# Turning a tail row's last 64 keys on VectorE instead of TensorE, and four planned durations of a list scheduler

## The chip, the cores and the metric

The kernel runs on one core of one Trainium2 chip. The metric is the device time of one execution in microseconds, in which every engine, queue and transfer counts.

## What is computed

The reference is causal attention with a decay, followed by a two-layer feed-forward network with a leaky activation.

```python
batch, n_heads, seq, head_dim = (8, 8, 576, 64)
scores = (1.0 / np.sqrt(D)) * np.matmul(q, k.transpose(0, 1, 3, 2))
cum = np.cumsum(np.log(np.clip(f, 0.0001, 1.0)), axis=-1)
scores = np.where(causal, -1000000000.0, scores + cum[:, :, :, None] - cum[:, :, None, :])
attn = softmax(scores)
x = np.matmul(attn, v).transpose(0, 2, 1, 3).reshape(4608, 512)
h = x @ w_in                                   # 512 -> 2048
out = (np.maximum(h, 0.0) + alpha * np.minimum(h, 0.0)) @ w_out   # 2048 -> 512
```

## The kernel before

The work is cut into 32 pairs of heads, `n` = 0 to 31, four for each batch element; a pair has 576 queries and 576 keys for two heads. The query rows of a head are four tiles of 128 and a tail of 64; the tails of both heads lie together in one tile of 128 rows. For each tile TensorE makes scores, VectorE adds the decay and finds the extreme (L826, for tails L663), ScalarE takes the exponential (L620). For the multiplication with `v` the weights of attention must lie with keys on partitions, so they are turned.

Pairs 0 to 7 are turned block by block on TensorE with an identity matrix (L634, L864), and ScalarE or VectorE copies the result from PSUM. Pairs 8 to 31 are called turned (`turned`, `NX`): their exponentials go into one buffer of 3,136 columns, `rE`. VectorE turns its first 3,072 columns in 32x32 squares, in four instructions of 768 columns into four buffers `rM` (L838). Sixteen DMAs a pair (L842), of 32 partitions x 768 columns each, on SP's queue and on GpSimd's, put the squares in place in a buffer `rTT`. There are two of these, one inside the tensor `big`, one inside `wr` (`wf`), so the profile shows the pairs by turns as `big<-big` and `wr<-big`.

The last 64 columns of that buffer, 3,072 to 3,136, are the tail rows' weights for keys 512 to 575. Those are turned on TensorE: one transpose a pair (L674), kept in the list `tails` until the next pair's visit, then a copy by ScalarE into 64 partitions of `rT4` (`eT`, L672). The other 64 partitions of `rT4` are zeros. So the matmul with `v` for this chunk, number 4 in `prods_of`, has 128 rows, of which 64 are zeros.

A value block (`prods_of`, L906) multiplies all chunks of both heads with `v`; the two heads go to the two halves of the output's partitions side by side. Each of these float32 matmuls appears as two instructions. In `visit`, TensorE first does the tail transpose of the pair before and the value block of the pair two before, and then three stages of scores: tiles 0 and 1, tile 2, tile 3. The tail's scores are made in `tail`, in two parts of 256 and 320 keys. In pairs 0 to 7 `stretch` makes the scores.

While attention runs, TensorE also works on the first layer of the network for earlier batch elements: `ffn1`, matmuls `bank<-xx,wi` of 512 columns, called x matmuls below, six an operation.

The order on every engine is made when the program is built, by a list scheduler (`Plan`): each operation has a planned duration in ns, a key, dependences and buffers, and each engine takes the operation that can start first, the lower key among equals. On TensorE x matmuls have late keys and stand where attention, by the plan, must wait. The chip runs each engine's list in that fixed order. Up to 82 us of planned time, a wait planned for TensorE of over 0.5 us is filled with matmuls on the identity (`fill`, L475).

Planned durations of TensorE's operations: `c_mm(n)` is the larger of 110 and 13.3 + 0.4175 n; `c_row(n, m)` is m times that; a value block of a turned pair is `ns_v` = 2,517 ns.

Of the kernel before, what the change touches and what calls it, by code (L numbers as in the profile page):

```python
# [12 lines left out]
U64 = mybir.dt.uint64  # L13
# [12 lines left out]
EW = 3072 + 64  # L26
NN = 8
# [191 lines left out]
def attention_moe(  # L219
# [65 lines left out]
    big = sp.tile([128, EW + 2 * 3072], F32, name="big")  # L285
# [9 lines left out]
    wr = sp.tile([128, 1904], U64, name="wr")  # L295
# [4 lines left out]
    cq = wf[:, 3072 : 3072 + 16 * GN].rearrange("p (s g) -> p s g", g=GN)  # L300
    rT4 = ring(sp, 2, [128, 128], F32, "eT4_")
# [14 lines left out]
    selt = sp.tile([128, 768], F32, name="sel")  # L316
    sel = selt[0:9].rearrange("p (i n) -> p i n", n=128)
# [125 lines left out]
    def select():  # L443

        po.memset(sel, 0.0)
        for i in range(4):
            for h in range(2):
                po.affine_select(sel[:, i, 64 * h : 64 * h + 64], sel[:, i, 64 * h : 64 * h + 64], pattern=[[0, 64]], base=-(i + 5 * h),
                                 channel_multiplier=1, compare_op=ALU.not_equal, fill=1.0)
        for h in range(2):  # L450
            po.affine_select(sel[:, 4 + h, 64 * h : 64 * h + 64], sel[:, 4 + h, 64 * h : 64 * h + 64], pattern=[[0, 64]], base=-4,
                             channel_multiplier=1, compare_op=ALU.not_equal, fill=1.0)
# [130 lines left out]
    waiting, behind, tails, later_x, quick_ops, value_ops, turn_ops = [], [], [], [], [], [], []  # L583

    def attention(n):
# [24 lines left out]
        bT4, bst = Buf(rT4), Buf(rst)  # L610
# [31 lines left out]
        tail_64 = (lambda t: t[:, 3072:3136]) if turned else (lambda t: t[:, 512:S])  # L642
        cut = (lambda ap: ap.rearrange("p (j c) -> p j c", c=64)) if turned else (lambda ap: ap)

        def tail(st):
# [5 lines left out]
            for g in range(2):  # L651
# [8 lines left out]
                s = op("PE", nt_ * c_mm(w_), prods, st + 0.6 * g, rdy, [bS] + held)  # L660
# [29 lines left out]
        def quick(bR, r_, key):  # L690
# [4 lines left out]
            def prods():  # L695
                R9 = bR.t[0:9]
                for i in range(4):
                    mm(at(128 * i), sel[:, i], R9, True, True)
                mm(at(512), sel[:, 4], R9[:, 0:64], True, False)
                mm(at(512), sel[:, 5], R9[:, 64:128], False, True)  # L700
# [47 lines left out]
        def visit(st):  # L748
# [3 lines left out]
            bt_, nt_p, turn_tail, tail_done = tails.pop() if tails else (None, None, None, None)  # L752
            go = rdy
            if after or bt_:
                vb, vp, vd, done = after() if after else ([Buf(rS)], lambda: None, [], lambda o: None)
                b_ = vb[1] if after else vb[0]

                def begin():
                    if bt_:
                        turn_tail(b_)  # L760
                    vp()
# [3 lines left out]
                if bt_:  # L765
                    tail_done(b_, a)
                if after:
                    value_ops.append(a)
                    done(a)
                    plan.at("A", n)  # L770
# [11 lines left out]
        def stretch(tiles, st):  # L782
# [8 lines left out]
            ns = 340 + sum(c_row(128 * i + 128, nt_) for i in tiles) + (ns_v if after else 0)  # L791
# [585 lines left out]
```

## Time and profile before

| | us |
|---|---|
| median of three runs | 1007.79 |
| the three runs | 1007.56 to 1009.26 |
| the profiled execution | 1008.97 |
| span of its instructions | 1007.2 |

The span runs from the first to the last instruction; 1.8 us of the profiled execution lie outside it. The profiled execution is 1.18 us above the median of the runs. In rows of the trace PE is TensorE's matmuls, PEld its weight loads, DVE VectorE, ACT ScalarE, POOL GpSimd, SP SyncE, and SPq what SyncE's queue issues. A matmul's own duration holds its way through the array, which overlaps with the next ones; the distance between two starts is what it takes from TensorE.

### The profile page before, as it was taken

Reading aid. Unit: us, or ns where it says so; the run is one execution under the profiler, and the core shown is the slowest. Engines: PE = TensorE matmul, PEld = TensorE weight load, DVE = VectorE, ACT = ScalarE, POOL = GpSimd, SP = SyncE. Lnnn points to the kernel's source line nnn. Section 1 sums busy time; section 2 is a strip of 40 time slices with the busy share of each in tenths; the row PEclk is TensorE's granted clock in tenths of the full one; section 3 lists DMA queues with packets and bytes.
Section 4 is the critical chain, followed back from the end, with each engine's and each line's share of the span. In section 5 each row is a group of like instructions: output and inputs, shape, how many; then the busy total and the mean of one; then the engine's idle time right before and its main releaser. Section 6 shows DMA issues by size and latency. Waiting matters only on the chain.

```text
span 1007.2 us, 22383 instructions
## 1 busy us (share of the span) xinstructions
PE 999.4 (99%) x7828; PEld 878.8 (87%) x7828; DVE 804.5 (80%) x1730; ACT 643.4 (64%) x1534; POOL 371.7 (37%) x625
## 2 busy tenths in 40 slices
PE   9999999999999999999999999999999999999998
PEld 5777878888888888888888888999999999999998
DVE  6898788887878867867628966698898988989994
ACT  7878977887777677767446746564554645546551
POOL 5465877889778788666240000000000000000000
PEclk9999999999999999999999999999999999999999
DMA  7877868888888888777746664643434344434411
GB/s 213 257 213 241 261 222 240 244 246 259 250 244 266 249 251 241 220 221 210 208 150 230 201 222 146 208 138 120 152 120 134 119 141 133 133 117 135 140 50 43
DMA packets 129535, 191.04 MB, mean 190 GB/s; under 512 B 22647, under 2 KB 75886, under 8 KB 129422
## 3 DMA queue, kind: packets, MB, share of 16 engines
q1 hardware_dynamic: 124526, 175.24, 56.3%
q0 software_dynamic: 4608, 14.16, 5.3%
q8 instruction: 62, 1.02, 0.4%
q14 instruction: 51, 0.42, 0.1%
q10 hardware_dynamic: 288, 0.20, 0.1%
HBM read 102.95 MB, written 48.67 MB: 151 GB/s over the span
## 4 chain that ended last, share of the span: by engine, by line
PE 95%; DMA 2%; DVE 2%; ACT 1%; SPq 0%; issue 0%; DVEq 0%
PE bank L378 92%; PE bank L634 2%; DMA Z<-c8p 1%; DMA ri<-rd 1%; PE bank L441 1%; DMA rd<-R 0%; ACT big L620 0%; DVE xs L927 0%; PE bank L674 0%; DVE big L826 0%; DVE big L629 0%; PE bank L717 0%; SPq L730 0%; PE bank L475 0%; ACT big L630 0%
## 5 line engine op out<-in xcount | busy, mean ns | idle before, releaser
L378 PE MATMUL bank<-xx,wi 128*128 128x512 f32 x1728 | 407.8, 393 | 0.0
L378 PEld LDWEIGHTS bank<-xx,wi 128*128 128x128 f32 x1728 | 320.5, 188 | 68.8 <-issue 1.7
L620 ACT ACTIVATE big<-big,st 128x384 f32<-128x384 f32 (+4 forms) x272 | 158.0, 583 | 26.1 <-DVE st L826 23.8
L826 DVE CUSTOM_DVE_ANT_0 big<-bank,Z 128x384 f32<-128x384 f32 (+1 forms) x220 | 93.0, 480 | 54.2 <-PE bank L378 45.6
L378 PE MATMUL bank<-wot,xx 128*128 128x256 f32 x1008 | 123.9, 283 | 0.0
L378 PE MATMUL bank<-wi,xx 128*128 128x256 f32 x1008 | 123.9, 283 | 0.0
L378 PEld LDWEIGHTS bank<-wi,xx 128*128 128x128 f32 x1008 | 122.3, 192 | 0.0
L378 PEld LDWEIGHTS bank<-wot,xx 128*128 128x128 f32 x1008 | 122.3, 192 | 0.0
L1021 DVE SCALAR_TENSOR_TENSOR hs<-bank,sa,hs 128x512 f32<-128x512 f32 x96 | 71.4, 744 | 42.8 <-ACT hs L1019 41.4
L1019 ACT ACTIVATE hs<-bank,ab 128x512 f32<-128x512 f32 x96 | 65.8, 685 | 53.2 <-PE bank L378 52.0
L533 POOL TENSOR_TENSOR Z<-Z,tri 128x128 f32<-128x128 f32 x192 | 78.1, 437 | 44.8 <-DVE Z L509 35.7
L838 DVE STREAM_TRANSPOSE big<-big 128x768 f32<-128x768 f32 x96 | 88.6, 953 | 2.6 <-ACT big L620 2.5
L1261 ACT ACTIVATE xx<-gx 128x1024 fp32r<-128x1024 f32 x48 | 50.8, 1058 | 30.8 <-PE bank L378 15.1
L931 POOL TENSOR_TENSOR xx<-xs,xx 128x256 fp32r<-128x256 f32 x64 | 48.9, 783 | 49.9 <-ACT xx L929 49.4
L1264 DVE TENSOR_TENSOR xx<-gx,xx 128x1024 fp32r<-128x1024 f32 x48 | 58.6, 1220 | 7.5 <-ACT xx L1261 7.5
L378 PE MATMUL bank<-wi,gh 128*128 128x256 f32 x504 | 62.4, 283 | 0.0
L378 PE MATMUL bank<-wot,gh 128*128 128x256 f32 x504 | 62.4, 283 | 0.0
L378 PEld LDWEIGHTS bank<-wot,gh 128*128 128x128 f32 x504 | 61.4, 192 | 0.1
L378 PEld LDWEIGHTS bank<-wi,gh 128*128 128x128 f32 x504 | 61.3, 192 | 0.0
L378 PEld LDWEIGHTS bank<-big,vr 128*64 128x64 f32 x1088 | 51.9, 137 | 9.2 <-issue 4.8
L378 PE MATMUL bank<-big,vr 128*64 128x128 f32 (+2 forms) x1088 | 59.7, 263 | 0.0
L1016 ACT ACTIVATE hs<-bank,sg 128x512 f32<-128x512 f32 x48 | 33.1, 689 | 41.2 <-PE bank L378 32.2
(165 smaller groups left out, 1704.0 us busy)
## 6 DMA issues: line engine op xcount, KB each, us to landing
hd<-hs SPq DMA_DIRECT2D x144, 256.0 KB, 3.4
wx<-hd SPq DMA_DIRECT2D x47, 512.0 KB, 3.6
rqk<-in_qk_dram SPq DMA_DIRECT2D x28, 512.0 KB, 5.5
hr<-hd SPq DMA_DIRECT2D x25, 512.0 KB, 3.7
big<-big SPq DMA_DIRECT2D x120, 96.0 KB, 3.1
wr<-big SPq DMA_DIRECT2D x120, 96.0 KB, 3.9
vr<-in_vv_dram SPq DMA_DIRECT2D x32, 320.0 KB, 3.6
wr<-in_w_in_dram SPq DMA_DIRECT2D x16, 512.0 KB, 6.0
```

The lines of the kernel that those rows point to most:

```text
L378: pe.matmul(o, lhsT, rhs, start=start, stop=stop)
L533: ms.append(op("POOL", c_po(128), lambda to=to, i=i, zd=zd: po.tensor_tensor(to()[:, :, -1:], zd()[:, :, i : i + 1], tk(), ALU.add), kc + ...
L620: ex = op("ACT", c_exp(w), lambda: ac.activation(at(bt.t), at(bt.t), AF.Exp, bias=lo()[:, col : col + 1], scale=-1.0, accum_out=su()[:, co ...
L634: pe.transpose(t[:, c : c + 128], src[:, 128 * j : 128 * j + 128], ident)
L826: ve.tensor_tensor_reduce(out=o if turned else blk(o), in0=blk(bS.t[:, c0 : c0 + w]), in1=in1(), scale=-0.125, scalar=3.0e38, op0=ALU.add, ...
L838: tn = op("DVE", c_tr(768), lambda k=k: ve.transpose(part(bm[k].t), part(bE.t[:, 768 * k : 768 * k + 768])), k0 + TK + k / 10, done, [bE, ...
L931: xl = op("POOL", c_po(256), lambda r=r, t0=t0: po.tensor_tensor(bx.t[:, 1, t0 : t0 + 256], bxs[r].t[:, 0:256], bx.t[:, 0, t0 : t0 + 256]. ...
L1016: cp = op("ACT", c_act(512), lambda bh=bh, bs=bs, fc=fc: ac.activation(bs.t, bh.t, AF.Copy, scale=sg[:, fc : fc + 1]), -1000, [last, o_sg] ...
L1019: cp = op("ACT", c_act(512), lambda bh=bh, bs=bs, fc=fc: ac.activation(bs.t, bh.t, AF.Relu, scale=ab[:, fc : fc + 1]), -1000, [last, o_sg] ...
L1021: cp = op("DVE", c_dve(512), lambda bh=bh, bs=bs, fc=fc: ve.scalar_tensor_tensor(bs.t, bh.t, sa[:, fc : fc + 1], bs.t, ALU.mult, ALU.add), ...
L1261: his.append(op("ACT", c_acs(128 * GW * (j1 - j0)), lambda j0=j0, j1=j1, src=src, o_=o_: ac.activation(o_(0, j0, j1), src(), AF.Copy), key ...
L1264: rdy.append(op("DVE", c_dve(128 * GW * (j1 - j0)), lambda j0=j0, j1=j1, src=src, o_=o_: ve.tensor_tensor(o_(1, j0, j1), src(), o_(0, j0, ...
```

## The change

- The transpose on TensorE and the copy by ScalarE go, for all 24 turned pairs. Turned pairs take no `rT4` any more.
- VectorE turns the 64 columns with the rest: the third of the four instructions is followed by another of 32 columns (3,104 to 3,136), and the fourth is 800 columns wide instead of 768 (3,072 to 3,104 come last in it).
- The buffers `rM` and `rTT` are 800 and 3,200 columns wide (`MW`). Of the 16 DMAs of a pair, the eight of the third and fourth buffer bring 800 columns, the others 768 as before.
- The keys 512 to 575 of a tail now lie on partitions 64 to 127 of `rTT`. The matmuls of chunk 4 use these 64 rows only, and the rows 64 to 127 of `v`; `v`'s two halves of 32 rows change places in the input for turned pairs.
- `rT4` and a part of the selection matrix `sel` move into `big`, to make room.
- Four planned durations: a tail's scores get 60 ns more; a value block in `visit` 400 more, where before 120 stood for the transpose and any value block had its bare time; the three stages of scores in `visit` get 290, 0 and 110 in place of 340, 0 and 0; a `stretch` of scores in pairs 0 to 7 gets -100 in place of 340.

```diff
+MW = 768 + 32
-    big = sp.tile([128, EW + 2 * 3072], F32, name="big")
+    big = sp.tile([128, EW + 8 * MW], F32, name="big")
-    wr = sp.tile([128, 1904], U64, name="wr")
+    wr = sp.tile([128, 1968], U64, name="wr")
-    rT4 = ring(sp, 2, [128, 128], F32, "eT4_")
+    rT4 = Ring(Store(cuts_of(9024, 2, 128)))
-        bT4, bst = Buf(rT4), Buf(rst)
+        bT4, bst = None if turned else Buf(rT4), Buf(rst)
...
-                s = op("PE", nt_ * c_mm(w_), prods, st + 0.6 * g, rdy, [bS] + held)
+                s = op("PE", nt_ * c_mm(w_) + 60, prods, st + 0.6 * g, rdy, [bS] + held)
...
             if turned:
-                def tail_done(b_, o):
-                    nonlocal e4
-                    e4 = op("ACT", c_act(128), lambda: ac.activation(bT4.t[0:64], b_.t[0:64, 384:512], AF.Copy), st + 1.31, [o], [b_, bT4])
-
-                tails.append((bt, nt, lambda b_: pe.transpose(b_.t[0:64, 384:512], tail_64(bt.t), ident), tail_done))
                 return bt, nt
...
-            bt_, nt_p, turn_tail, tail_done = tails.pop() if tails else (None, None, None, None)
             go = rdy
-            if after or bt_:
...
-                a = op("PE", 120 + (ns_v if after else 0), begin, st, rdy + vd + ([nt_p, o_id] if bt_ else []),
-                       vb + ([bt_] if bt_ else []), need=(rS, len(vb[:2]) + 4))
...
+            if after:
+                vb, vp, vd, done = after()
+                a = op("PE", ns_v + 400, vp, st, rdy + vd, vb, need=(rS, len(vb[:2]) + 4))
...
-                s = op("PE", (340 if g == 0 else 0) + c_row(w_, nt_), lambda part=part: rows_of_scores(part), -3000, got, bS[g] + held, glue=1.5)
+                s = op("PE", (290, 0, 110)[g] + c_row(w_, nt_), lambda part=part: rows_of_scores(part), -3000, got, bS[g] + held, glue=1.5)
...
-            ns = 340 + sum(c_row(128 * i + 128, nt_) for i in tiles) + (ns_v if after else 0)
+            ns = (340 if n >= NN else -100) + sum(c_row(128 * i + 128, nt_) for i in tiles) + (ns_v if after else 0)
...
                     for k in range(4):
-                        tn = op("DVE", c_tr(768), lambda k=k: ve.transpose(part(bm[k].t), part(bE.t[:, 768 * k : 768 * k + 768])), k0 + TK + k / 10, done, [bE, bm[k]])
+                        w_ = MW if k >= 2 else 768
+
+                        def turn(k=k):
+                            c0, b_ = 768 * k, bm[k].t
+                            ve.transpose(part(b_[:, 0 : 768 if k < 3 else MW]), part(bE.t[:, c0 : c0 + (768 if k < 3 else MW)]))
+                            if k == 2:
+                                ve.transpose(b_[:, 768:MW], bE.t[:, 3104:3136])
+
+                        tn = op("DVE", c_tr(768) + (0, 0, 130, 33)[k], turn, k0 + TK + k / 10, done, [bE, bm[k]])
...
-                                bTT.t[32 * k : 32 * k + 32, 768 * a : 768 * a + 768], bm[k].t[32 * a : 32 * a + 32]), k0 + 8 + j / 100, [tn], [bm[k], bTT], kb=96))
+                                bTT.t[32 * k : 32 * k + 32, MW * a : MW * a + w_], bm[k].t[32 * a : 32 * a + 32, 0:w_]), k0 + 8 + j / 100, [tn], [bm[k], bTT], kb=w_ / 8))
...
-                                        + [(4, 256, 320, bT4.t[:, 64 * h : 64 * h + 64])] + [(j, 256, 320, tt_of(x3(j, 0), 2 * h, 2 * h + 2)) for j in range(4)])
+                                        + [(4, 256, 320, tt_of(768, 2 * h, 2 * h + 2)[64:128])] + [(j, 256, 320, tt_of(x3(j, 0), 2 * h, 2 * h + 2)) for j in range(4)])
...
-                        mm(o_.rearrange("p (a r) -> p a r", r=32) if len(m.shape) == 3 else o_, bv.t[:, j, h], m, c in first, c in last)
+                        mm(o_.rearrange("p (a r) -> p a r", r=32) if len(m.shape) == 3 else o_, bv.t[128 - m.shape[0] :, j, h], m, c in first, c in last)
...
-        if n == B * NP - 1:
-            bt_, nt_p, turn_tail, tail_done = tails.pop()
-            b_ = Buf(rS)
-            tail_done(b_, op("PE", 109, lambda: turn_tail(b_), k0 + 9, [nt_p, o_id], [b_, bt_]))
```

## Rows read from the trace of the kernel before

**Rows 1.** The page's first two parts: busy time of the engines with their share of the span, then TensorE's granted clock in 40 equal slices, in tenths of full speed.

```profile
PE 999.4 (99%) x7828; PEld 878.8 (87%) x7828; DVE 804.5 (80%) x1730; ACT 643.4 (64%) x1534; POOL 371.7 (37%) x625
...
PEclk9999999999999999999999999999999999999999
```

**Rows 2.** Busy time by stage: start and end in us, length, then each engine's busy us, granted clock, the DMA engines' busy share and GB/s.

```profile
core 0: us, PE busy (x) PEld busy (x) DVE busy (x) ACT busy (x) POOL busy (x), PEclk, DMA share, GB/s
40.00:60.00 20.00, 18.67 (x202) 14.56 (x202) 19.54 (x49) 14.40 (x43) 16.34 (x20) 1.00 0.72 209
147.00:157.00 10.00, 8.64 (x41) 6.60 (x39) 8.90 (x22) 8.66 (x24) 7.57 (x13) 1.00 0.81 236
157.00:495.00 338.00, 338.00 (x2895) 281.04 (x2895) 264.77 (x655) 247.34 (x717) 254.70 (x440) 1.00 0.83 240
495.00:980.00 485.00, 485.00 (x3565) 460.10 (x3564) 399.20 (x718) 260.50 (x443) 15.02 (x21) 1.00 0.46 149
```

**Rows 3.** The chain of work that ended last, in order of time: start, length in us, and what.

```profile
123.17 7.12 DMA Z<-c8p
130.36 4.90 DMA rd<-R
136.42 3.65 DMA ri<-rd
...
147.60 0.60 DVE xs L927
...
495.70 507.93 PE bank L378 x3756
```

**Rows 4.** The tail transposes of turned pairs (L674) and the copies behind them (L672): engine, operation, count; shortest, median and longest ns, first and last start, shape.

```profile
L674 PE MATMUL bank<-ident,big x24: 270/270/271, 140.8 to 493.9; 128*64 128x128 f32 x24
...
L672 ACT ACTIVATE eT<-bank x24: 255/259/272, 142.8 to 494.3; 64x128 f32<-64x128 f32 x24
```

**Rows 5.** TensorE's matmuls in order of time (start us, us from the first start to the last end, instruction, count), in three stretches: a row of x matmuls up to a tail transpose; a transpose and the value block behind it; value work that follows x matmuls with no transpose between.

```profile
221.64 5.63 PE L378 MATMUL bank<-xx,wi 128*128 128x512 f32 x24
...
226.42 0.84 PE L378 MATMUL bank<-xx,wi 128*128 128x512 f32 x3
227.10 0.27 PE L674 MATMUL bank<-ident,big 128*64 128x128 f32 x1
227.30 0.33 PE L378 MATMUL bank<-wr,vr 128*64 128x128 f32 x2
...
507.57 0.84 PE L378 MATMUL bank<-xx,wi 128*128 128x512 f32 x3
508.34 0.33 PE L378 MATMUL bank<-wr,vr 128*64 128x128 f32 x2
```

**Rows 6.** The same view inside that value block, up to the scores behind it, with one row of weight loads (PEld; in brackets the idle time before). The figures after the tensors are the active rows and columns of the array, then partitions x columns streamed.

```profile
228.45 0.61 PE L378 MATMUL bank<-wr,vr 128*64 128x128 f32 x8
228.88 0.28 PE L378 MATMUL bank<-eT,vr 128*64 128x64 f32 x4
229.00 0.23 PE L378 MATMUL bank<-wr,vr 128*64 128x64 f32 x2
...
229.79 0.50 PE L378 MATMUL bank<-wr,vr 128*64 128x128 f32 x6
230.22 0.33 PE L378 MATMUL bank<-Kh,Qh 64*128 64x128 f32 x2
...
231.78 0.39 PE L378 MATMUL bank<-Kl,Qh 64*128 64x512 f32 x2
232.01 0.40 PE L378 MATMUL bank<-Kh,Ql 64*128 64x512 f32 x2
232.34 0.50 PE L378 MATMUL bank<-xx,wi 128*128 128x512 f32 x1
...
232.34 0.30 PEld L378 LDWEIGHTS bank<-xx,wi 128*128 128x128 f32 x2 [0.36 <-ACT big L620]
```

**Rows 7.** The same view where tile 2's scores (384 columns) are followed by tile 3's (512) at once, and at the first (x matmuls alone) and the last of the four places where x matmuls stand between.

```profile
231.37 0.34 PE L378 MATMUL bank<-Kh,Ql 64*128 64x384 f32 x2
231.55 0.40 PE L378 MATMUL bank<-Kh,Qh 64*128 64x512 f32 x2
...
291.98 0.50 PE L378 MATMUL bank<-xx,wi 128*128 128x512 f32 x1
...
484.83 0.34 PE L378 MATMUL bank<-Kh,Ql 64*128 64x384 f32 x2
485.10 1.65 PE L378 MATMUL bank<-xx,wi 128*128 128x512 f32 x6
486.68 0.50 PE L378 MATMUL bank<-Kh,Qh 64*128 64x512 f32 x2
```

**Rows 8.** The filler matmuls (L475) as a group and ten of them in order of time with what follows, the first x matmuls, and TensorE's wait near 149 us.

```profile
L475 PE MATMUL bank<-ident x30: 275/275/377, 40.3 to 54.4; 128*128 128x128 f32 x30
...
46.29 1.28 PE L475 MATMUL bank<-ident 128*128 128x128 f32 x10
47.50 0.71 PE L378 MATMUL bank<-rqk 64*128 64x128 f32 x6
...
59.98 3.02 PE L378 MATMUL bank<-xx,wi 128*128 128x512 f32 x12
...
149.31 0.41 PE L378 MATMUL bank<-Kh,Qh 128*128 128x320 f32 x1 [1.36 <-DVE st L826]
```

**Rows 9.** VectorE's turning by width, as groups of instructions (count, busy us, mean ns of one), and its longest wait between 157 and 495 us (total us, times, longest).

```profile
L838 DVE STREAM_TRANSPOSE big<-big 128x768 f32<-128x768 f32 x96 | 88.6, 953 | 2.6 <-ACT big L620 2.5
L509 DVE STREAM_TRANSPOSE Z<-wr 128x1024 f32<-128x1024 f32 x22 | 27.3, 1240 | 0.0
L511 DVE STREAM_TRANSPOSE Zt<-sel 128x576 f32<-128x576 f32 x22 | 16.5, 750 | 0.0
...
DVE big L826 <- PE bank L378: 42.8, 23, 5.3
```

**Rows 10.** The pair's DMAs near 255 us: the last issues on SP's queue, how long transfers of L842 took to land between 253.5 and 259.2 us (shortest, median, longest), and TensorE at the value block that reads them.

```profile
253.11 3.13 SPq L842 DMA_DIRECT2D wr<-big  x5
...
DMA to landing us min/median/max: 3.2/4.7/6.1
...
258.66 0.27 PE L674 MATMUL bank<-ident,big 128*64 128x128 f32 x1
258.86 0.55 PE L378 MATMUL bank<-wr,vr 128*64 128x128 f32 x6
```

More of the change, by code (lines that the diff above doesn't have):

```diff
@@ L299, in attention_moe @@
     GN = B * H - G0
-    cq = wf[:, 3072 : 3072 + 16 * GN].rearrange("p (s g) -> p s g", g=GN)
-    rT4 = ring(sp, 2, [128, 128], F32, "eT4_")
+    cq = wf[:, 4 * MW : 4 * MW + 16 * GN].rearrange("p (s g) -> p s g", g=GN)
+    rT4 = Ring(Store(cuts_of(9024, 2, 128)))
     rst = ring(sp, 3, [128, 28], F32, "st")
@@ L315, in attention_moe @@
     wbf = wf[:, 0:256].bitcast(BF16)
-    selt = sp.tile([128, 768], F32, name="sel")
-    sel = selt[0:9].rearrange("p (i n) -> p i n", n=128)
+    selt = sp.tile([128, 704], F32, name="sel")
+    sel = [selt[0:9, 128 * i : 128 * i + 128] for i in range(4)] + [big[0:9, 9280 + 128 * i : 9408 + 128 * i] for i in range(2)]
     cl = selt[0 : B * H, 0:S]
@@ L443, in select @@
     def select():
-        po.memset(sel, 0.0)
+        po.memset(selt[0:9, 0:512], 0.0)
+        po.memset(big[0:9, 9280:9536], 0.0)
         for i in range(4):
             for h in range(2):
-                po.affine_select(sel[:, i, 64 * h : 64 * h + 64], sel[:, i, 64 * h : 64 * h + 64], pattern=[[0, 64]], base=-(i + 5 * h),
+                po.affine_select(sel[i][:, 64 * h : 64 * h + 64], sel[i][:, 64 * h : 64 * h + 64], pattern=[[0, 64]], base=-(i + 5 * h),
                                  channel_multiplier=1, compare_op=ALU.not_equal, fill=1.0)
         for h in range(2):
-            po.affine_select(sel[:, 4 + h, 64 * h : 64 * h + 64], sel[:, 4 + h, 64 * h : 64 * h + 64], pattern=[[0, 64]], base=-4,
+            po.affine_select(sel[4 + h][:, 64 * h : 64 * h + 64], sel[4 + h][:, 64 * h : 64 * h + 64], pattern=[[0, 64]], base=-4,
                              channel_multiplier=1, compare_op=ALU.not_equal, fill=1.0)
@@ L581, in load_n @@
         return out, rz, rt, bZ, [(Qh, Kh), (Qh, Kl), (Ql, Kh)]
-    waiting, behind, tails, later_x, quick_ops, value_ops, turn_ops = [], [], [], [], [], [], []
+    waiting, behind, later_x, quick_ops, value_ops, turn_ops = [], [], [], [], [], []
     def attention(n):
@@ L641, in attention @@
         tail_of = (lambda t: t.rearrange("p (m c) -> p m c", c=64)[:, 0:49:6]) if turned else (lambda t: t)
-        tail_64 = (lambda t: t[:, 3072:3136]) if turned else (lambda t: t[:, 512:S])
+        tail_64 = lambda t: t[:, 512:S]
         cut = (lambda ap: ap.rearrange("p (j c) -> p j c", c=64)) if turned else (lambda ap: ap)
@@ L697, in prods @@
                 for i in range(4):
-                    mm(at(128 * i), sel[:, i], R9, True, True)
-                mm(at(512), sel[:, 4], R9[:, 0:64], True, False)
-                mm(at(512), sel[:, 5], R9[:, 64:128], False, True)
+                    mm(at(128 * i), sel[i], R9, True, True)
+                mm(at(512), sel[4], R9[:, 0:64], True, False)
+                mm(at(512), sel[5], R9[:, 64:128], False, True)
             q_ = op("PE", 1400, prods, key, [r_, o_sel], bB + [bR])
@@ L751, in visit @@
             after = behind.pop(0) if len(behind) > 1 else None
-            bt_, nt_p, turn_tail, tail_done = tails.pop() if tails else (None, None, None, None)
             go = rdy
-            if after or bt_:
[L755 to L761, printed above, removed]
-                a = op("PE", 120 + (ns_v if after else 0), begin, st, rdy + vd + ([nt_p, o_id] if bt_ else []),
-                       vb + ([bt_] if bt_ else []), need=(rS, len(vb[:2]) + 4))
[L765 to L770, printed above, removed]
+            if after:
+                vb, vp, vd, done = after()
+                a = op("PE", ns_v + 400, vp, st, rdy + vd, vb, need=(rS, len(vb[:2]) + 4))
+                value_ops.append(a)
+                done(a)
+                plan.at("A", n)
                 go = [a]
@@ L955, in values @@
             todo = [prods_of(r, lambda r=r: bP[r].t) for r in (1, 0)]
-            return (bP + [bv] + bT1 + bT2 + [bT3, bT4], lambda: [f_() for f_ in todo], v_deps(),
+            return (bP + [bv] + bT1 + bT2 + ([bT3] if turned else [bT3, bT4]), lambda: [f_() for f_ in todo], v_deps(),
                     lambda o: [done_v(r, bP[r])(o) for r in (1, 0)])
@@ L1043, in spread_rows @@
             src = cl[32 * g : 32 * g + 32].rearrange("p (s r) -> p s r", r=32)
-            out_ = wf[0:32, 3072 + 32 * g : 3072 + 32 * g + 16 * GN].rearrange("p (k s g) -> p k s g", k=4, s=4)[:, :, :, 0:32]
+            out_ = wf[0:32, 4 * MW + 32 * g : 4 * MW + 32 * g + 16 * GN].rearrange("p (k s g) -> p k s g", k=4, s=4)[:, :, :, 0:32]
             ve.transpose(out_, src[:, 0:16].rearrange("p (s k) r -> p k s r", k=4))
@@ L1066, in swap1 @@
     def swap1():
-        more(rM.store, *cuts_of(EW, 4, 768))
-        more(rTT.store, big[:, EW + 3072 :])
+        more(rM.store, *cuts_of(EW, 4, MW))
+        more(rTT.store, big[:, EW + 4 * MW :])
     def swap2():
-        more(rTT.store, wf[:, 0:3072])
+        more(rTT.store, wf[:, 0 : 4 * MW])
         more(rhs.store, hs[:, 3])
@@ L1353 @@
     vp = v.reshape(B, NP, 2, S, D).transpose(0, 1, 3, 2, 4)
-    vp = np.concatenate([vp, vp[:, :, S - 64 :]], axis=2).reshape(B, NP, 5, 128, 2, D).transpose(0, 1, 3, 2, 4, 5)
+    va, vb = vp[:, :, S - 64 : S - 32], vp[:, :, S - 32 :]
+    late = (np.arange(B * NP) >= NX[0]).reshape(B, NP, 1, 1, 1)
+    vp = np.concatenate([vp, np.where(late, vb, va), np.where(late, va, vb)], axis=2).reshape(B, NP, 5, 128, 2, D).transpose(0, 1, 3, 2, 4, 5)
     qkrow = np.concatenate([qrow, krow], axis=-1)
```

2 lines of the change are left out of this document (1 added, 1 removed).

## The prediction, made before the changed kernel was run

> **What bounds the kernel now.** I read the page's first two parts, then the busy times by stage. TensorE is busy 99% of the span at full clock [rows 1]. By stage it is short of work in two places only, before 60 us and around 147 us; from 157 to 980 us it has none to spare [rows 2]. The chain of waits says the same: one piece of TensorE work runs from 495.70 us almost to the end, and what is not TensorE lies between 123 and 149 us, where DMAs that fetch `Z`, `rd` and `ri` and the multiplication of `xs` come last [rows 3]. A busy TensorE need not run at its peak, so I use distances between starts of matmuls. The steady x-times-w_in matmul takes (227.10 - 221.64) / 24 = 0.2275 us [rows 5]. So in the stage with the changed pairs, whatever TensorE is given more or less to do moves the end by as much, and what VectorE, ScalarE or a queue does counts only if it makes TensorE wait.
>
> **Part 1: 24 transposes leave TensorE.** Each tail transpose is one matmul with its weight load, 24 in all [rows 4]. Its row says 0.27 us, but that is a pipelined length. Compare two entries into a block of value matmuls: three x matmuls, the transpose, then the first value matmul take 227.30 - 226.42 = 0.88 us; three x matmuls and then directly the value matmul take 508.34 - 507.57 = 0.77 us [rows 5]. The transpose is worth 0.11 us. 24 x 0.11 = **-2.6 us**.
>
> **Part 2: the last 64 keys become a 64-row block in the middle of a 128-row stream.** Before, the chunk of `eT` is multiplied with 128 active rows, half of them zeros, in the shape 128*64 of its neighbours. After, it is partitions 64 to 127 alone: four matmuls of shape 64*64 between chunks of 128*64, in every turned pair. Rows show what a change of shape costs. Within value work, eight matmuls (four steps of two heads side by side) take 228.88 - 228.45 = 0.43 us, 0.108 a step; the last three steps ahead of the scores (64*128) take 230.22 - 229.79 = 0.43, so 0.10 is extra. Scores step by 0.23, but 0.33 into 128*128: 0.10 extra [rows 6]. The x matmuls step by 0.2275, but the three ahead of value work take 0.77 instead of 0.68: 0.09 extra [rows 5]. So a change of rows alone, of columns alone, or of both costs 0.09 to 0.10 us, and the weight load behind it has idle time ahead of it, 0.36 us in the place shown [rows 6]. The new block has one change in and one out: 2 x 0.095 x 24 = **+4.6 us**. From below: the 64*64 shape appears nowhere in this trace, and if it runs as part of the 128*64 stream the price is 0; the matmuls themselves have the same 64 columns as now (four in 229.00 - 228.88 = 0.12 us [rows 6]). I take the full price, because all three kinds that do appear pay it.
>
> The Trainium skill says so as a rule: TensorEngine Tiling (Array Packing), section Tiling Modes, lists 128x64 and 64x64 as different configurations and states that "changing tiling mode (not just tile) drains the TensorE". The trace agrees for the shapes it has, with the 0.09 to 0.10 us above; whether this block counts as a change no row of before shows. By the rule parts 1 and 2 together give +2.0 us, without it -2.6.
>
> **Part 3: work that lies beside TensorE.** ScalarE loses 24 copies of 0.259 us, 6.2 us [rows 4]. VectorE's 32x32 turning took 1.240 us for 1,024 columns and 0.750 for 576, so 1.09 ns a column over 0.12 us; 768 columns took 0.953 [rows 9]. The extra instruction of 32 columns is then 0.12 + 0.035 = 0.155 us, the 32 further columns of the last cut 0.035: 0.19 us a pair, 4.6 us over 24 pairs. VectorE is idle 338 - 265 = 73 us of that stage [rows 2], 42.8 of them waiting for TensorE itself [rows 9]. I count both at **0**; with no such cover VectorE's 4.6 us would come on top.
>
> Half of the pair's 16 transfers grow from 96 to 100 KB, and the first starts no later, the last two groups 0.155 to 0.19 us later. Behind them wait the pair's own value matmuls. In the tightest pair I found, the last of five issues on SP ended near 256.3 us, transfers there took 3.2 to 6.1 us to land (median 4.7), and value work began at 258.86, 0.20 us behind its transpose, as at 227.30, so without a wait [rows 10]. The transfer grows by 4%, some 0.2 us of 4.7. The planner is given the longer VectorE time and the larger size, and puts the value block after as many x matmuls as it needs. I take **0**; without that cover it is 0.19 + 0.2 = 0.4 us a pair in the few tight pairs, 2 us for five of them.
>
> **Part 4: four planned durations.** They change no instruction, only the order. A value block was planned with the transpose at 2,637 ns and is now 2,917 without it; the trace has 230.22 - 227.30 = 2.92 us [rows 5, 6]. The score stages go from 521 + 340, 521, 681 to 521 + 290, 521, 681 + 110. After 157 us TensorE is never idle, so a better order has no wait to remove there. It can change how often x matmuls stand between two stages of scores. In four places, the first at 291.98 and the last at 485.10 us, x matmuls split the 512-wide stage from the one before [rows 7]. A split costs two changes of shape: 485.10 - 484.83 = 0.27 and 486.68 - 485.10 = 1.58 for six x matmuls, against 0.18 unsplit (231.55 - 231.37) and 6 x 0.2275 = 1.37 [rows 7]: 0.30 us. Fewer splits give at most 4 x 0.30 = -1.2 us, a split in the 18 other pairs of that stage +5.4. Planned ends that are later leave more time for banks to come free, so I take half of the gain, **-0.6**.
>
> In the first 60 us it matters more. Planned TensorE time of a score stage of pairs 0 to 7 falls by 440 ns, while a tail grows by 60 twice. The plan there puts in filler matmuls (`fill`, L475) where it believes TensorE to wait: 30 rows of 0.12 us (ten of them in 47.50 - 46.29), 3.6 us [rows 8]. VectorE has 19.54 of 20 us busy from 40 to 60 us [rows 2], so the stretch ends with its work. Bounds: all filler time and the 1.36 us wait at 149 us [rows 8] gone, -5.0; as many fillers again as the 12 stages of pairs 0 to 3 become shorter in the plan, 12 x 0.44 - 8 x 0.06 = +4.8. I take **0**, in the middle, as the fillers stand where VectorE makes TensorE wait anyway.
>
> **Sum:** -2.6 + 4.6 + 0 + 0 - 0.6 + 0 = +1.4 us, on the profiled execution 1008.97 to 1010.4. That execution is 1.18 above the median of the runs, 1007.79; set against the median the sum gives 1009.2, which I forecast. 0.2% is 2.0 us, about what a measurement of this kernel can tell from no change; the forecast, 1.4 us, is within it.
>
> **Rivals.**
> *No change of shape is paid.* For it: the neighbours stand in the same two column halves, and the rows used are part of theirs. Against it: every change of rows in the trace is paid. Then -2.6 - 0.6 = -3.2: 1004.6 us, faster.
> *The start gets more fillers* (the other side: slower). Place: L475 before 60 us, from a plan that believes in shorter score stages. Every new filler row that TensorE had work for costs 0.12 us; 17 rows more are +2.0 us by themselves, and beside part 2 six (+0.7) carry the sum past 2.0. For it: the planned times fall by 5 us. Against it: VectorE is full there, so fillers stand in true idle time. With 17 rows: 1009.2 + 2.0 = 1011.2; at its bound 1014.0.
> *The start gets tighter.* The planned durations come nearer to the traced ones and the chain of `ri` and `xs` up to 149 us [rows 3] is issued earlier. Then up to -5.0; with two thirds of it 1009.2 - 3.3 = 1005.9, which is no change against the median, or faster by more.
> *The corrected plan does nothing,* because TensorE is full: -2.6 + 4.6 alone, 1009.8, inside the forecast.
>
> **How the numbers follow.** Forecast (shape paid, order neutral, the last rival included) 0.58, by itself 1007 to 1012, of which 0.07 faster, 0.55 within 0.2%, 0.38 slower. No shape price 0.20 (three quarters faster, the rest the same). More fillers or late landings 0.12 (0.85 slower). Tighter start 0.10 (0.6 faster). Together: faster 0.04 + 0.15 + 0.06 = 0.25; same 0.32 + 0.05 + 0.02 + 0.04 = 0.43; slower 0.22 + 0.10 = 0.32. The range reaches to the second rival's middle and past the first's time by part of the gain at the start: 1003.8 to 1012.6.
>
> **What would show it.** Part 1: no transposes after 157 us and x matmuls 0.32 us ahead of value work. Part 2: the step from the last 128-column value matmul to the first of shape 64*64 is 0.20 instead of 0.10 us, the step out 0.15 instead of 0.05, and the value block takes 3.11 us up to the scores; 2.92 would make the prediction wrong by 4.6 us. Part 3: no wait of a value weight load for a DMA. Part 4: the count of L475 rows, the time of the first x matmul (59.98 us now, [rows 8]) and the wait at 149 us tell which rival of the start it was.

## The result and the profile after

The changed kernel takes 1015.0 us (1014.34 to 1015.87), beside 1008.14 for the kernel before: ratio 1.0069, 95% interval 1.0053 to 1.0085. It is slower, by 6.9 us, and lies outside the forecast range. The profiled execution took 1015.87 us with a span of 1014.1, again 6.9 more than before.

The page's first two parts answer [rows 1]:

```profile
PE 1005.1 (99%) x7794; PEld 877.5 (87%) x7794; DVE 806.4 (80%) x1754; ACT 637.9 (63%) x1510; POOL 372.2 (37%) x626
...
PEclk9999999999999999999999999999999999999999
```

TensorE has 34 matmul instructions fewer (24 transposes, 10 fillers) and is busy 5.7 us longer. By stage, as [rows 2] (start and end, length, busy us of each engine, granted clock, DMA share, GB/s):

```profile
40.00:60.00 20.00, 18.84 (x189) 14.24 (x187) 17.91 (x49) 14.36 (x44) 11.73 (x18) 0.91 0.84 205
54.00:56.00 2.00, 1.86 (x4) 0.84 (x4) 1.82 (x9) 1.84 (x6) 2.00 (x4) 0.58 1.13 262
56.00:58.00 2.00, 2.00 (x23) 1.94 (x24) 1.71 (x9) 1.82 (x6) 1.80 (x4) 0.57 1.09 228
147.00:157.00 10.00, 9.08 (x43) 7.32 (x42) 9.68 (x29) 7.79 (x24) 8.28 (x18) 1.00 0.92 222
157.00:495.00 338.00, 336.70 (x2848) 275.51 (x2848) 264.52 (x675) 242.81 (x696) 257.72 (x443) 1.00 0.82 240
495.00:980.00 485.00, 485.00 (x3536) 458.48 (x3535) 396.06 (x710) 258.35 (x444) 14.77 (x22) 1.00 0.47 152
```

Two things are new. The granted clock, 1.00 in every stage before, is 0.58 and 0.57 between 54 and 58 us: at the lower level (1.2 of 2.4 GHz) for (0.42 + 0.43) x 2 / 0.5 = 3.4 us, which costs up to 1.7 us. And TensorE, never idle between 157 and 495 us before, now is for 1.3 us there. The timeline of TensorE shows both places, and between them a value block that answers [rows 5, 6] (start, us from the first start to the last end, in brackets the idle time before):

```profile
52.43 0.55 PE L379 MATMUL bank<-R,big 9*128 9x64 f32 x4
54.14 1.99 PE L379 MATMUL bank<-rqk 64*128 64x384 f32 x4 [1.16 <-DVE st L811]
...
224.67 1.52 PE L379 MATMUL bank<-xx,wi 128*128 128x512 f32 x6
226.12 3.28 PE L379 MATMUL bank<-big,vr 128*64 128x128 f32 x60
229.33 0.33 PE L379 MATMUL bank<-Kh,Qh 64*128 64x128 f32 x2
229.50 0.27 PE L379 MATMUL bank<-Kl,Qh 64*128 64x128 f32 x2
...
355.55 0.61 PE L379 MATMUL bank<-xx,wi 128*128 128x512 f32 x2
357.33 3.28 PE L379 MATMUL bank<-wr,vr 128*64 128x128 f32 x60 [1.17 <-DVE big L829]
```

The transpose is gone: six x matmuls and then the value block take 226.12 - 224.67 = 1.45 us, which is five steps of 0.2275 and 0.31 into the block. The block takes 229.33 - 226.12 = 3.21 us up to the scores, 0.29 longer than before. The row at 226.12 joins three shapes under the name of the first; here are starts of single instructions inside it, one for each step of two heads:

```
227.479  128*64, 128 columns
227.588  128*64, 128 columns   +0.109
227.798   64*64,  64 columns   +0.210
227.904   64*64,  64 columns   +0.106
228.059  128*64,  64 columns   +0.155
228.166  128*64,  64 columns   +0.107
228.224  128*64,  64 columns   +0.058
```

Each change of shape is paid twice: about 0.10 us at the first step in the new shape (0.210 for 0.109, 0.155 for 0.058) and 0.05 more at the second (0.106 and 0.107 for 0.058). In and out, that is 0.295 us a pair.

The fillers (answering [rows 8]) and VectorE's turning (as [rows 9]), as groups: count, shortest, median and longest ns, first and last start:

```profile
L477 PE MATMUL bank<-ident x20: 273/275/377, 18.3 to 41.9; 128*128 128x128 f32 x20
...
L829 DVE STREAM_TRANSPOSE big<-big x24: 164/169/172, 148.9 to 498.9; 128x32 f32<-128x32 f32 x24
```

Twenty fillers instead of 30, and all before 42 us instead of 40 to 54: none stands any more where TensorE waits near 53 us. Of the other signs named for the start, the first x matmul begins at 59.76 us (59.98 before), and the wait of 1.36 us near 149 us is one of 0.92 us at 148.83:

```profile
148.83 1.42 PE L379 MATMUL bank<-xx,wi 128*128 128x512 f32 x5 [0.92 <-ACT hs L1005]
```

The last rows of SP's queue ahead of the value block that waits at 357.33:

```profile
351.28 0.51 SPq L835 DMA_DIRECT2D wr<-big  x1
351.89 1.82 SPq L727 DMA_DIRECT2D ri<-rd  x3
353.75 1.22 SPq L835 DMA_DIRECT2D wr<-big  x2
```

The pair's last two transfers are issued behind three of `ri`, the last near 354.4 us. The block starts 2.9 us later, after 1.17 us of idle time. The row names VectorE's short turning as what ended the wait, but it was the transfers. In the trace's semaphore events the last of them has landed at 357.20 us, 2.8 us after its issue; TensorE's queue passes its two waits for the transfers at 356.89 and 357.28 (below; count, ns, first and last start) and starts the block's first weight load 0.02 us later. The short turning belongs to the next pair. It ends at 357.29 and reports at 357.30, at the very start of that load; where VectorE does end a wait, at 54.14, the load starts 0.04 us behind its report.

```profile
L379 PEldq EVENT_SEMAPHORE  x2: 51/51/51, 356.8 to 357.2; - x2
```

### The profile page after: what moved, and what is told of

It is laid out like the page before. It is cut to its first block, busy times and chain, and to the rows that moved or that the text cites. A ratio compares the mean times of both kernels' runs of the same rounds, so it can differ in the third digit from the quotient of the medians.

```text
span 1014.1 us, 22324 instructions
## 1 busy us (share of the span) xinstructions
PE 1005.1 (99%) x7794; PEld 877.5 (87%) x7794; DVE 806.4 (80%) x1754; ACT 637.9 (63%) x1510; POOL 372.2 (37%) x626
## 4 chain that ended last, share of the span: by engine, by line
PE 97%; DMA 1%; DVE 1%; ACT 1%; SPq 0%; issue 0%; DVEq 0%; ACTq 0%
PE bank L379 93%; PE bank L636 2%; DMA ri<-rd 1%; PE bank L442 1%; ACT big L622 0%; PE bank L714 0%; PE bank L477 0%; DVE xs L920 0%; SPq L727 0%; DVE big L631 0%; ACT hs L1008 0%; ACT big L632 0%; PE bank L857 0%; ACT hs L1005 0%; DVE big L827 0%
## 5 line engine op out<-in xcount | busy, mean ns | idle before, releaser
L535 POOL TENSOR_TENSOR Z<-Z,tri 128x128 f32<-128x128 f32 x192 | 80.3, 450 | 31.0 <-DVE Z L511 24.8
L379 PEld LDWEIGHTS bank<-big,vr 128*64 128x64 f32 (+1 forms) x1168 | 55.2, 138 | 13.2 <-issue 6.8
L379 PE MATMUL bank<-big,vr 128*64 128x128 f32 (+2 forms) x1168 | 64.0, 264 | 0.0
```

The lines of the kernel that those rows point to most:

```text
L379: pe.matmul(o, lhsT, rhs, start=start, stop=stop)
L535: ms.append(op("POOL", c_po(128), lambda to=to, i=i, zd=zd: po.tensor_tensor(to()[:, :, -1:], zd()[:, :, i : i + 1], tk(), ALU.add), kc + ...
```

## Experiments

The theory from these rows: the shape costs 24 x 0.295 = 7.1 us instead of 4.6, the transposes give back 2.6, and the four durations cost the other 2 to 3 us, by half clock and late value blocks. Rivals: the wider turning delays the value blocks by itself; or the durations are harmless and the moved turning disturbed the start.

### The two halves of the change

**turn_only** has the moved turning and the four durations as before; **times_only** is the kernel before with the four corrected durations (400 ns for the block beside its transpose).

```diff
 # turn_only, against the changed kernel
-s = op("PE", nt_ * c_mm(w_) + 60, prods, ...)
+s = op("PE", nt_ * c_mm(w_), prods, ...)
-a = op("PE", ns_v + 400, vp, ...)
+a = op("PE", 120 + ns_v, vp, ...)
-s = op("PE", (290, 0, 110)[g] + c_row(w_, nt_), ...)
+s = op("PE", (340, 0, 0)[g] + c_row(w_, nt_), ...)
-ns = (340 if n >= NN else -100) + sum(...)
+ns = 340 + sum(...)
```

> The changed kernel with all four planned durations as they were. Theory A (the 64-row block costs two changes of shape, 0.15 us each in the trace of after, 7.1 us over 24 pairs, against 2.6 us for the transposes): +4.5 us on before, 1012.6. Theory B (most of the 6.9 us is the new order: half clock near 55 us, waits): at most +2 us, 1010 or less. Either by 1 us, as the order still moves a little.

> The kernel before with the four corrected durations and the transposes left on TensorE. Theory A: the rest of the 6.9 us, +2.4, 1010.5, with a stretch at half clock before 60 us. Theory B: +5 us or more, 1013.

turn_only took 1012.22 us, ratio 1.0043 [1.0031, 1.0055]: +4.35 for the +4.5 worked out, with 30 fillers, full clock, and no wait of a value block. So the wider turning and the larger transfers cost nothing that shows within the interval, some 1.2 us either way. The agreement is better than was earned: the wait of 1.36 us near 149 us ([rows 8]), which that sum left alone, is gone in turn_only. The other 2.8 us of the changed kernel (2.6 by the two ratios) come with the durations. times_only took 1011.23 us, 1.0035 [1.0022, 1.0048], +3.4, and its runs lay far apart (1009.08 to 1014.92). It has the 20 fillers, up to 40.8 us, and the wait near 53 us, but not the half clock that was expected behind it:

```profile
53.06 1.25 PE L378 MATMUL bank<-rqk 64*128 64x384 f32 x4 [1.15 <-DVE st L826]
...
40.00:60.00 20.00, 18.68 (x194) 1.00 0.80 214
```

(The second row is a stretch: start and end, length, TensorE's busy us, granted clock, DMA share, GB/s.) Its two longest waits between 157 and 495 us (total us, times, longest) are of value blocks for late transfers, this time by name: a pair's turned weights, and the load of `v`.

```profile
PE bank L378 <- DMA wr<-big: 2.0, 1, 2.0
PE bank L378 <- DMA vr<-in_vv_dram: 1.8, 1, 1.8
```

The longer of them ends at 347.87, and the clock is low behind it (0.52 from 349 to 351 us). The durations make fewer fillers and late value blocks in a kernel in which no turning was moved. Both rivals fall.

### Chunk 4 on 128 rows, the lower 64 zero

The lower 64 rows of the chunk in both `rTT` buffers are set to zero once by GpSimd, and chunk 4 uses all 128 rows. The result is the same, and no shape changes in the block.

```diff
-+ [(4, 256, 320, tt_of(768, 2 * h, 2 * h + 2)[64:128])] + ...
++ [(4, 256, 320, tt_of(768, 2 * h, 2 * h + 2))] + ...
...  # value blocks of turned pairs also depend on `low`
+for t_, d_ in ((big[0:64, EW + 4 * MW :], o_swap), (wf[0:64, 0 : 4 * MW], o_swap2)):
+    low.append(op("POOL", 300, lambda t_=t_: po.memset(t_.rearrange("p (a x) -> p a x", a=4)[:, :, 768:MW], 0.0), 0, [d_]))
```

> The changed kernel, but chunk 4 runs with all 128 rows: the 64 rows below are set to zero once in each buffer, so that the shape stays 128*64. Theory A: the 7.1 us go, 1015.0 - 7.1 = 1007.9, and no 64*64 matmuls stand in the trace. Theory B: 1013 or more, since the order is that of after.

> As zero_rows, with the four planned durations as they were. Theory A: only the transposes are gone, -2.6 us on before, 1005.5, faster than both kernels. Theory B, or a hidden cost of the turning on VectorE and its DMAs: 1008 or more.

zero_rows, with the new durations, took 1013.78 us, 1.0057 [1.004, 1.0074]: 6 us over its expectation, which had only the shape in it. Its runs lay between 1010.83 and 1017.05 us; the profiled one took 1016.15. The waits of TensorE after 60 us took the gain back (total us, times, longest):

```profile
PE bank L379 <- DVE big L830: 3.0, 1, 3.0
PE bank L379 <- DMA wr<-big: 2.1, 1, 2.1
PE bank L379 <- ACT hs L1006: 1.7, 1, 1.7
```

The first two are of value blocks, the third is of an x matmul near 150 us. Half clock stands behind the first, whose row names VectorE's turning as the one at 357.33 did and which ended at 419.56 us (0.52 from 420 to 422 us), and at the start as in the changed kernel. My reading is that with shorter value blocks TensorE comes to the next one earlier, so that the transfers are later still. **zero_rows_old**, the same with the durations as before, took 1006.53 us, 0.9983 [0.9974, 0.9993]; waits of value blocks of 1.7 and 0.3 us were left.

### More planned time for transfers

`LAG` is the time that the planner gives a turned pair's transfers to land, ahead of the pair's value block. It changes no instruction, only the order.

```diff
-LAG = 2000
+LAG = 4000      # lag_after, zero_rows_lag; 3500 in zero_old_lag, turn_lag, before_lag
```

> The changed kernel with the plan's allowance for the landing of a pair's transfers (LAG) at 4,000 ns instead of 2,000. Theory A (the longer planned durations took away a lead that TensorE's lateness gave the transfers): no wait of a value block for them, 1.5 to 2.5 us less than after, 1012.5 to 1013.5, and less spread between runs. Theory B: waits stay or go elsewhere, 1014 or more.

> zero_rows (128 rows, corrected durations) with LAG at 4,000 ns. zero_rows took 1013.8 with waits of 0.9, 2.3, 0.4 and 3.1 us of value blocks. Theory A (late transfers ate the 7.1 us that the shape gave back): these waits go and with them the half clock behind them, 1007.5 to 1009.5. Theory B: 1012 or more.

> zero_rows_old (128 rows, durations as before) with LAG at 3,500 ns. It took 1006.5 with waits of 0.4, 0.5 and 1.9 us near 380 and 412 us. Theory A: the waits go and the whole 2.6 us of the transposes stays, 1004.5 to 1005.5. Theory B: the order gets worse elsewhere, 1006.5 or more.

lag_after took 1014.01 us, 1.0054 [1.0041, 1.0066], 1.0 less than the changed kernel; more was expected, and the two intervals overlap. The waits of value blocks are gone, and the start with its half clock is as it was. Of its five executions the one with a mean granted clock of 1.000 took 1012.22 us, the four at 0.996 to 0.998 took 1013.95 to 1014.71. zero_rows_lag took 1007.53, 0.9995 [0.9986, 1.0004]: against zero_rows 6.3 us less. Its trace keeps the half clock at the start and the wait of 1.7 us near 150; gone are the waits of value blocks (6.0 us in zero_rows) and the half clock behind the longest, so these were the loss. zero_old_lag (zeros, old durations, 3500) took **1004.72 us**, 0.996 [0.9946, 0.9973], with no listed wait of TensorE after 60 us and full clock: 3.5 us better than the kernel before.

**turn_lag** is the same with the 64-row block, **before_lag** the kernel before with 3500:

> The change with the four planned durations as before, and the planner's extra time for transfers (LAG) 3500 ns instead of 2000, as in the kernel with zero rows and old durations that took 1004.7 us. It differs from that kernel only in the shape of chunk 4 (64 rows instead of 128 with zeros). If the change of shape costs 2 x 0.15 us a pair and nothing else differs, 1004.7 + 24 x 0.296 = 1011.8 us, with no value block waiting. If instead the missing lead of the transfers made part of what turn_only lost (1012.2), it comes out at 1009 us or lower.

> The kernel before with LAG 3500 instead of 2000 and nothing else. The kernel with 128 rows in chunk 4, zeros in the lower 64, the old durations and LAG 3500 took 1004.7 us; this one has the 24 transposes on TensorE instead, so if LAG helps both alike it takes 1004.7 + 24 x 0.11 = 1007.3 us, and the removed transposes are the gain. If LAG alone made that gain, it takes about 1004.7 as well; if LAG does nothing to the old kernel, which has no stalled value block, 1008.2.

turn_lag took 1011.89 us, 1.0038 [1.0024, 1.0051]: 7.2 us over zero_old_lag for the shape alone, where 24 x 0.296 = 7.1 was worked out. Its value block up to the scores takes 226.27 - 223.06 = 3.21 us:

```profile
223.06 3.28 PE L379 MATMUL bank<-big,vr 128*64 128x128 f32 x60
226.27 0.33 PE L379 MATMUL bank<-Kh,Qh 64*128 64x128 f32 x2
```

and that of zero_old_lag 225.84 - 222.92 = 2.92 us:

```profile
222.92 2.99 PE L379 MATMUL bank<-big,vr 128*64 128x128 f32 x60
225.84 0.33 PE L379 MATMUL bank<-Kh,Qh 64*128 64x128 f32 x2
```

before_lag took 1006.78 us, 0.9988 [0.9979, 0.9997]. Against it zero_old_lag is 2.1 us faster by the medians, and 2.8 when each is set against the runs of the kernel before that were taken with it; the rest of the 3.5 us is `LAG`'s. In the two pages TensorE is busy 2.4 us less, near the 2.6 forecast for the transposes:

```profile
PE 999.2 (99%) x7828; PEld 879.2 (87%) x7828; DVE 804.1 (80%) x1730; ACT 643.5 (64%) x1534; POOL 371.5 (37%) x625
...
PE 996.8 (99%) x7804; PEld 876.7 (87%) x7804; DVE 806.4 (80%) x1754; ACT 639.3 (64%) x1510; POOL 373.4 (37%) x628
```

The wait of 1.36 us near 149 us stands in before_lag, too, and not in zero_old_lag; why it went was not tested. The two spans, 1007.2 and 1003.2 us, differ by more than the medians, so the transposes' gain is known to about 1 us.

### One change of shape instead of two

**one_change** is turn_lag with chunk 4 as the last chunk ahead of the scores.

```diff
-+ [(4, ...[64:128])] + [(j, 256, 320, ...) for j in range(4)]
++ [(j, 256, 320, ...) for j in range(4)] + [(4, ...[64:128])]
-todo = [prods_of(r, ...) for r in (1, 0)]
+todo = [prods_of(r, ...) for r in ((0, 1) if turned else (1, 0))]
```

> As turn_lag, but in a turned pair's value block chunk 4 (64 rows) is the last chunk of the last half instead of the first, so that the scores (64*128) follow it at once: the sequence 128*64, 64*64, 64*128 has one change more than 128*64, 64*128, where turn_lag's has two more. If a change costs 0.15 us whatever its kind, half of the price goes: 1004.7 + 24 x 0.148 = 1008.3 us. If a change of rows and one of columns cost separately (128*64 to 64*128 pays both already), the last step is cheaper and it comes out near 1005 to 1006.5. If the price is one of the 64*64 shape itself, 1011.8 as turn_lag.

It took 1008.25 us, 1.0002 [0.9993, 1.0011], 3.6 less than turn_lag: half of the price. The block takes 226.36 - 223.30 = 3.06 us:

```profile
223.30 3.13 PE L379 MATMUL bank<-big,vr 128*64 128x128 f32 x60
226.36 0.33 PE L379 MATMUL bank<-Kh,Qh 64*128 64x128 f32 x2
```

So the price goes by changes; it isn't the 64*64 shape that is dear. Into the scores the first step is 0.10 us too long whether columns alone change (from 64*64, 226.361 - 226.206 = 0.155 for 0.058) or rows and columns (from 128*64 in zero_old_lag, 225.841 - 225.632 = 0.209 for 0.109).

### Which duration

**start_old** is the changed kernel with the stretch at 340 again. **only_stretch**, **only_block** and **only_stages** are turn_only with one correction each: the stretch at -100; the block at 400; the tail's 60 with the stages' 290, 0, 110 (the lines of the first diff, the other way round).

> The changed kernel with only the planned duration of the score stages of pairs 0 to 7 back at 340; value blocks, scores and tails keep the corrected ones. Theory A (the start at half clock comes from this duration alone): 30 filler rows and full clock before 60 us again, 1.5 to 2.5 us less than after, 1012.5 to 1013.5, with waits of value blocks for late transfers left. Theory B (the start is not what differs): as after, 1014 to 1016.

> The kernel with the moved turning and the durations as before (turn_only, 1012.2 us), with one duration of the change: a stretch of pairs 0 to 7 at -100 instead of 340. If this one causes the start of the changed kernel: 20 fillers that end before 42 us in place of 30, a wait of 1.3 us near 53 us and half the granted clock for 3.4 us behind it, no late value block after 200 us, and about 1012.2 + 1.7 = 1013.9 us. If the start needs the other durations too, 30 fillers, full clock and 1012.2 us.

> turn_only (1012.2 us) with one duration of the change: a value block in visit 400 ns over its bare time instead of 120. If the block's duration was the lead that hid late transfers, value blocks wait after 200 us as in the changed kernel (1.3 us in one place there) while the start stays as in turn_only, 30 fillers and full clock: 1013 to 1014.5 us, with more spread between runs. If the lead came from elsewhere, no value block waits and it takes 1012.2 us.

> turn_only (1012.2 us) with the other two durations of the change: 60 ns more for a part of a tail's scores and 290, 0, 110 for the three stages. A pair is planned 60 to 180 ns longer, against 280 by the block's duration, so less lead is lost: at most one value block waits by over 0.3 us, full clock at the start, 1012.0 to 1013.0 us. If these two are what takes the lead, value blocks wait as in the changed kernel and it takes 1013.5 us or more.

start_old took 1022.29 us, 1.0136 [1.0116, 1.0156], where 1013 was expected. The start had full clock, as forecast, but TensorE then waited 4.53 us at one place and half clock followed from about 156.8 us (0.69 from 156 to 158, 0.50 from 158 to 160 us). A second wait, 2.2 us near 241 us, had half clock behind it, too (0.53 from 242 to 244 us). The first:

```profile
156.43 0.51 PE L379 MATMUL bank<-xx,wi 128*128 128x512 f32 x1 [4.53 <-ACT xx L922]
```

One duration taken back made another order with another hole; taken alone, that run could say nothing of the start.

only_stretch took 1016.03 us, 1.008 [1.0067, 1.0093], +3.8 on turn_only. It has the start of the changed kernel: 20 fillers up to 42.0 us, a wait of 1.15 us up to 54.19, and no value block waits later. The columns of its stretches are start and end, length, TensorE's busy us, granted clock, DMA share, GB/s:

```profile
54.00:56.00 2.00, 1.81 (x4) 0.50 0.49 115
56.00:58.00 2.00, 2.00 (x19) 0.50 0.76 246
58.00:60.00 2.00, 2.00 (x30) 0.50 0.03 8
60.00:62.00 2.00, 2.00 (x21) 0.79 0.00 0
```

The low level lasts (3 x 0.50 + 0.21) x 2 / 0.5 = 6.8 us here, up to 3.4 us lost, most of the 3.8. The executions bear this out: the one with a mean granted clock of 1.000 took 1013.35 us, the other four, at 0.997 and 0.998, took 1016.02 to 1017.21. So the stretch's duration alone makes that start, with its fillers and its wait; whether the clock falls behind the wait differs between executions of one kernel. only_block took 1012.35 us, 1.0046 [1.0034, 1.0059], as turn_only, and no value block waits: the expectation that this one takes the lead from the transfers is wrong. only_stages took 1019.61 us, 1.0119 [1.0104, 1.0134], where about 1012.5 was expected. No value block waits, but around 147 us, where VectorE's work comes last ([rows 3, 8]), there is a hole, with half clock behind it (0.85 from 151 to 153, 0.50 from 153 to 155 us):

```profile
144.67 2.43 PE L379 MATMUL bank<-xx,wi 128*128 128x512 f32 x10
151.05 0.39 PE L379 MATMUL bank<-Kh,Qh 128*128 128x256 f32 x1 [3.95 <-DVE st L811]
```

The effects do not add up: +3.8, +0.1 and +7.4 alone, +2.8 together.

### Work for the wait near 53 us

**lag_warm** is lag_after with six identity matmuls planned behind the matmuls with 9 active rows (`bank<-R,sel`) that stand ahead of that wait.

```diff
+bF = Buf(rT)
+op("PE", 1300, lambda: [pe.matmul(bF.t[:, 0:128], ident, ident, start=True, stop=True) for _ in range(6)], key, [q_], [bF])
```

> The change with LAG 4000 (as lag_after, 1014.0 us), with six identity matmuls into a bank of their own put in a score stretch of pairs 0 to 7, planned at 1300 ns, so that TensorE has work at the wait of 1.3 us near 53 us after which the granted clock was 0.5 for 3.4 us. If that wait makes the clock fall, the clock stays full through 60 us and it takes 1.7 us less than lag_after, about 1012.3 us. If the clock falls for another reason, half clock shows at 54 us again and the time is 1014.0 or more by the added matmuls.

It took 1017.3 us, 1.009 [1.0076, 1.0105], and did not test what it was for. The scheduler put the matmuls elsewhere (their group: shortest, median, longest ns, first and last start), and the wait stayed, yet the clock stayed full behind it.

```profile
L702 PE MATMUL bank<-ident x12: 275/275/377, 63.0 to 64.3; 128*128 128x128 f32 x12
```

The wait, on the timeline:

```profile
53.72 1.25 PE L379 MATMUL bank<-rqk 64*128 64x384 f32 x4 [1.15 <-DVE st L813]
```

The granted clock by stretches, in the columns above:

```profile
54.00:56.00 2.00, 1.83 (x20) 1.00 1.12 256
56.00:58.00 2.00, 2.00 (x46) 1.00 1.08 236
142.00:144.00 2.00, 0.70 (x3) 1.00 0.12 46
144.00:146.00 2.00, 1.28 (x4) 0.72 0.55 133
```

The same 1.15 us wait is followed by 1.2 GHz in lag_after's trace and by 2.4 GHz in this one, as in times_only's. Here the clock fell near 145 us instead, after two waits of 1.30 and 0.72 us. What decides it, these rows don't tell.

## Why the prediction was wrong

**Part 1, the transposes: right.** None is left, and the way from x matmuls into the block is 0.31 us where 0.32 was forecast. That is the forecast 0.11 us a pair, 2.6 in all; before_lag against zero_old_lag gives 2.1 by the medians and 2.4 by TensorE's busy time.

**Part 2, the change of shape: right in kind, mis-sized.** The prediction named the two steps, 0.20 and 0.15 us, and they came. The term was too small: it took the first step in a new shape for the whole price. The second is 0.05 us longer as well, so the price is 2 x 0.148 x 24 = 7.1 us where +4.6 stood; 2.5 us of the miss. The forecast 3.11 us for the block was 3.21. The pattern was to be seen before, but only the entry was read: at the direct entry into value work of [rows 5] the steps start at 508.338, 508.498 and 508.607 us, so behind the long entry comes one of 0.160 and only then the 0.109 of the stream. turn_lag against zero_old_lag confirms 7.1 with 7.2, and one_change that it goes by changes. The Trainium skill's rule (TensorEngine Tiling (Array Packing), section Tiling Modes), that a new mode drains the engine, agrees: each change costs 0.148 us here, though no row shows the draining itself. The rival "no shape price" fell.

**Part 3, work beside TensorE: right for the work that the change adds.** The short turning took 0.169 us (0.155 forecast), and turn_only shows no wait for VectorE or the larger transfers. The sign named for it, no value block waiting for a DMA, was broken in the changed kernel, at 357.33 us, but by Part 4: turn_lag and lag_after have the same shape and the same transfers and no such wait.

**Part 4, the four durations: wrong, 3.4 us of the miss.** It gave -0.6 for the order and 0 for the start; against turn_only the changed kernel has +2.8. X matmuls stand between tiles 2 and 3 in three places instead of four, which by the forecast's price is worth 0.3 us and comes with turn_only too. Two steps of the argument failed.

*"A better order has no wait to remove there"* was right; that a worse one can bring a wait was not priced. With all four durations the value block at 357.33 meets its transfers 1.2 us early, and more time for transfers in the plan removes the wait (the 1.0 us by which lag_after is faster is not clear of the noise). A reading that fits all of this: the old durations were too short by up to 0.46 us a pair (280 + 60 + 120 ns), so TensorE ran behind its plan, and transfers had a lead that stood nowhere in the plan. The part of it that the runs show is that all durations together take it and LAG gives it back; only_block and only_stages each left it. How much a single one takes is open.

*"The fillers stand where VectorE makes TensorE wait anyway."* The rival of more fillers was the wrong way round: ten fewer came, and earlier. The wait they had filled, 1.16 us at 54.14, stood open, and the clock fell behind it. That is 1.7 us, and no part of the forecast had the clock in it. only_stretch shows that the stretch's duration makes the wait, and all four executions of the changed kernel have a mean granted clock of 0.996 to 0.998. With 1.2 us at 357.33 that makes 2.9 of the 2.8 us, but there are more terms, which cancel. The changed kernel also waits 0.25 and 0.31 us near 66 and 0.92 at 148.83 us; turn_only waits 0.54 and 0.78 us near 53 us and runs ten fillers more, 1.2 us. Together 1.7 + 1.17 + 1.16 + 0.56 + 0.92 - 1.32 - 1.2 = 3.0 us, the difference of the two spans (1014.1 and 1011.1).

Set against the miss of 5.8 us: 2.5 and 3.4, with the baseline 0.35 us higher over all runs, are 6.2; the rest is within the spread of the runs, and of about the size of the 1.36 us wait near 149 us that went in turn_only without a term in the sum.

## What to carry to other kernels

Price a change of matmul shape over all steps until the old spacing is back, not over the first; and where a short block would break the shape, zeros in the unused rows kept the block at 2.92 us and saved 7 us here. A planned duration that is wrong may be what keeps transfers ahead and fills a hole: correct it together with the planned time of the transfers, and look for new waits at each, as a corrected plan is another order and not a better one. Before changing several planner inputs, run each alone and all together, for their effects don't add.

## What was not expected of the hardware

A wait of TensorE of about 1.2 us could cost more than itself. Seven traces have it, 1.15 to 1.16 us behind the same few matmuls with 9 active rows. The granted clock was at the lower level behind it for 3.4 us in the changed kernel, lag_after and zero_rows, for 6.8 us in only_stretch and zero_rows_lag, and not at all in times_only and lag_warm. It differs between executions of one kernel as well: one of five in lag_after, one of five in only_stretch and two of eleven in zero_rows_lag had a mean granted clock of 1.000, the others less. So one trace says what such a wait cost in that execution and not what it costs.

The changes of shape cost the same 0.15 us from 128*64 to 64*64 and from there back to 128*64, and the first step from 64*64 to the scores' 64*128 has the same 0.10 us in it.
